# A fused attention and two-MLP kernel on one core: the second pass's attention starts earlier and is spread wider

## The chip, the cores and the metric

The kernel runs on one core of a Trainium2 chip. That core has a matrix engine (TensorE, PE in the profile), a vector engine (VectorE, DVE), a scalar engine (ScalarE, ACT), a GpSimd engine (POOL), and SyncE (SP), whose queue issues all the DMAs here. Each engine works through its own instructions strictly in order; a semaphore tells it when another engine's result is there. The metric is the device time of one execution in microseconds (us), lower is better.

## The reference

```python
kv  = einsum('bhsd,bhse->bhde', k, v)            # B, H, S, D = 8, 8, 576, 64
out = einsum('bhsd,bhde->bhse', q, kv)
x = out / sqrt(mean(out*out, -1) + 1e-6) * g_norm  # -> (4608 tokens, 512)
h = x @ w_in                                     # 512 -> 2048
x = (relu(h) + log1p(exp(-abs(h)))) @ w_out      # softplus, 2048 -> 512
h = max(x @ w1, x @ w2, x @ w3)                  # 512 -> 768
y = h @ w_out2                                   # 768 -> 512
```

Everything is float32. The attention has no softmax: for each batch a 64 x 64 matrix `kv` per head is made once and every query is multiplied by it; then each head's output is normalized.

## The kernel before

The 4608 tokens go through in five passes (`NS`: twice 464 tokens in each of the first four, twice 448 in the last). A pass holds its activations transposed, features on the partitions and tokens along the row, in two token halves. Every dense layer is worked as 2 x 2 block products with seven multiplications instead of eight (numbered 1, 5, 6, 2, 7, 4, 3 in their order of work); one "group" (`run_group`) is the seven products of one pair of weight rows, and each product is two matmuls of 128x128 by 128x464 (two records per matmul in the trace in the first pass, so four records a product).

The first pass multiplies in plain float32 and prepares the weights on the way: a raw block is loaded (`load_raw`, three buffers), turned into float32 by two ScalarE and two VectorE instructions (`rebase`, `join`; tiles `raw`, `cv`, `sw`), four sums of blocks are formed on GpSimd (`sums_of_weights`, `sw`), then each sum is split into a high and a low part (`make_unit`: ScalarE casts, GpSimd subtracts, tiles `u`, four buffers) and written to DRAM (`keep_first`, tiles `wd`) for the later passes. Those multiply three times with high and low parts (`mm3`).

Order is written by hand. Every step is put on a list with a time in "slots" (`at(t, fn, ...)`); one group is 7 slots. The list is sorted, and a scheduler keeps nearly this order on each engine; SyncE's order is pinned to it in this part. In the first pass, groups 0 to 7 are the first layer (`Xh`, `Yh`, `Wh` in PSUM), groups 8 to 15 the second layer (`Xx`, `Yx`, `Wx`; the last four, here called X20, X21, X30 and X31, start at slots 84, 91, 98 and 105), groups 16 to 24 the three-way layer (`Xo`, `Yo`, `Wo`; nine groups from `base2` = slot 119 on), and the output layer begins at slot 184. In the second layer every product is added to the running sums by VectorE (`x2`); in the three-way layer ScalarE first copies three or four products of a group out of PSUM (`m`), and the next product of the same bank cannot begin before that copy.

Beside the three-way layer runs the next pass's attention (`attention_beside`). For each of the two new batches, k and v of four head pairs are loaded (`load_kv`, two pairs of buffers), multiplied (`kv_mm`, `kvps`), and copied and split (`kv_evict`: `kvh`, `kvl`). Then come eight steps, one for each token half and head pair, numbered k = 0 to 7 here:

- `load_q` and `split_q`: `qh` by ScalarE, `ql` by GpSimd for even pairs and by VectorE for odd ones;
- `out_mm`: six short matmuls into `o`;
- `square`: on ScalarE the square `sq`, the scaled copy `og` and the cast `sh`; the low part `sl` again on GpSimd for even pairs, on VectorE for odd ones;
- `ssq_mm`: two matmuls `ss`, of `sh` and of `sl`, with a matrix of ones;
- `norm`: ScalarE `r`, `r`, `t`; VectorE `t`, `r`; GpSimd multiplies `og` by `r`.

At the end `combine_x` splits the eight `og` into the operands of the second pass (`hi`, `lo`).

Of the kernel before, what the change touches and what calls it, by code (L numbers as in the profile page):

```python
# [48 lines left out]
def kernel(  # L49
# [111 lines left out]
    def at(t, fn, *args):  # L161
        events.append((t, len(events), fn, args))
# [381 lines left out]
    rt, tt = {}, {}  # L544
# [98 lines left out]
    def new_batches(pas, t):  # L643

        a = TOK[pas] + t * NS[pas]
        first = -1 if a == 0 else (a - 1) // S
        return list(range(first + 1, (a + NS[pas] - 1) // S + 1))

    def attention_beside(pas, t0):

        n = NS[pas]

        for t, tt, dts in ((0, t0 - 9, (0, 2, 6, 9)), (1, t0 + 16, (0, 3, 6, 9))):
            for b in new_batches(pas, t):

                for p in range(NP):
                    at(tt + (dts[p] - 10 if p < 2 else dts[p - 2] + 0.15), load_kv, b, p)
                    at(tt + dts[p] + 0.1, kv_mm, b, p)
                at(tt + dts[3] + (0.2 if t == 0 else 1.35), kv_evict, b)
        for k in range(2 * NP):  # L660
            h, p = divmod(k, NP)
            a = TOK[pas] + h * n
            t = t0 + 8 + 6 * k
            at(t - 6, load_q, a, n, p)
            at(t - 3, split_q, a, n, p)
            at(t + 0.3, out_mm, a, n, p)
            at(t + 0.4, square, a, n, p)
            at(t + 4.8, ssq_mm, a, n, p)
            at(t + 4.9, norm, a, n, p)

    def run_pass(pas, base):
# [140 lines left out]
        if pas + 1 < NPASS:  # L812
            attention_beside(pas + 1, base2)
            for s, ms in enumerate(STEPS):
                at(base3 + 5 + SLOT[ms[-1]] + 0.5, combine_x, pas + 1, (s,))
# [87 lines left out]
    for k in range(-1, 2 * NP + 2):  # L903
        t = OPEN + 3 * (k + 1)
# [145 lines left out]
```

## Time and profile before

| | us |
|---|---|
| three runs, median (lowest to highest) | 1412.64 (1410.28 to 1413.76) |
| the profiled execution's own time | 1412.19 |
| its span, first to last instruction | 1410.4 |
| busy in the span: PE, DVE, ACT, POOL | 1388.8, 810.3, 747.2, 727.8 |

The profile's engines are PE, PEld (weight loads, which overlap PE), DVE, ACT, POOL and SP. A timeline row gives the start, the length, the engine, the line of the kernel, the operation and the tiles (written <- read), the shape, how many equal records were merged, and in brackets the idle time before it with the instruction that ended it. Instructions overlap a little at their ends, so the step from one start to the next is the better price where an engine is busy.

### The profile page before, as it was taken

What the parts mean: (1) busy time and instruction counts of PE and PEld (TensorE: products, weight loads), DVE (VectorE), ACT (ScalarE), POOL (GpSimd) and SP (SyncE); (2) the same over time, 40 slices, a digit from 0 to 9 for tenths busy, and PEclk for the clock granted to TensorE, in tenths of its full rate; (3) what the DMA queues carried; (4) which work ended last, traced back from release to release, by engine and by line L of the source; (5) the groups of instructions that cost most, each with busy time, mean ns of one, the idle gap of its engine ahead of it and who ended that gap; (6) DMA issues with size and microseconds to landing.
All of it is one profiled execution on the core that took longest, in us unless ns stands there. A gap on an engine that the chain in (4) does not pass through costs nothing.

```text
span 1410.4 us, 18509 instructions
## 1 busy us (share of the span) xinstructions
PE 1388.8 (98%) x6098; PEld 1111.6 (79%) x6098; DVE 810.3 (57%) x1283; ACT 747.2 (53%) x1427; POOL 727.8 (52%) x666
## 2 busy tenths in 40 slices
PE   8899999999999999999999999999999999999998
PEld 5344455544688888888888898888888889999898
DVE  5655566667355575764456567554475764456544
ACT  6766646665375545754543566464446754543332
POOL 3898787865364464544434444443364534444320
PEclk9999999999999999999999999999999999999999
DMA  7587778756699986667666875766676667666665
GB/s 278 188 285 277 275 273 329 248 196 210 222 321 332 316 306 214 213 206 267 209 209 209 268 247 188 258 221 209 209 218 208 212 200 269 220 214 210 211 219 180
DMA packets 122142, 336.51 MB, mean 239 GB/s; under 512 B 13120, under 2 KB 33472, under 8 KB 122048
## 3 DMA queue, kind: packets, MB, share of 16 engines
q1 hardware_dynamic: 122048, 335.33, 71.2%
q8 instruction: 49, 0.80, 0.2%
q14 instruction: 45, 0.37, 0.1%
HBM read 269.88 MB, written 65.40 MB: 238 GB/s over the span
## 4 chain that ended last, share of the span: by engine, by line
PE 87%; DMA 4%; ACT 3%; POOL 2%; DVE 2%; issue 1%; SPq 0%; POOLq 0%; ACTq 0%
PE Xo L136 4%; PE Xo L137 4%; PE Xo L138 4%; PE Xx L136 4%; PE Xx L138 4%; PE Xx L137 4%; PE Xh L136 4%; PE Xh L137 4%; PE Xh L138 4%; PE Xx L372 3%; PE Xo L372 2%; PE Xh L372 2%; PE Yo L138 2%; PE Yo L137 2%; PE Yo L136 2%; PE Yh L136 2%
## 5 line engine op out<-in xcount | busy, mean ns | idle before, releaser
L126 POOL TENSOR_TENSOR lo<-e,hi 128x464 fp32r<-128x464 f32 (+1 forms) x160 | 188.2, 1209 | 186.0 <-ACT hi L120 175.4
L120 ACT CAST hi<-t 128x464 fp32r<-128x464 f32 (+1 forms) x120 | 65.4, 545 | 118.3 <-DVE e L132 47.2
L126 POOL TENSOR_TENSOR u<-sw,u 128x512 fp32r<-128x512 f32 (+1 forms) x92 | 109.8, 1218 | 28.0 <-ACT u L120 27.9
L120 ACT COPY m<-Xo 128x464 f32<-128x464 f32 (+1 forms) x135 | 72.7, 544 | 82.5 <-PE Xo L138 73.9
L129 DVE TENSOR_TENSOR x<-x,Xx 128x464 f32<-128x464 f32 (+1 forms) x120 | 75.4, 631 | 55.5 <-PE Xx L138 51.2
L132 POOL TENSOR_TENSOR e<-e 128x464 f32<-128x464 f32 (+1 forms) x40 | 47.4, 1185 | 100.3 <-DVE t L132 93.2
L120 ACT CAST hi<-e 128x464 fp32r<-128x464 f32 (+1 forms) x160 | 85.0, 580 | 20.3 <-PE Yx L137 17.0
L126 DVE TENSOR_TENSOR lo<-t,hi 128x464 fp32r<-128x464 f32 (+1 forms) x120 | 75.7, 634 | 34.3 <-ACT hi L120 31.5
L136 PE MATMUL Xo<-hi,u 128*128 128x464 f32 (+1 forms) x224 | 84.7, 379 | 0.6 <-ACT m L120 0.5
L137 PE MATMUL Xo<-lo,u 128*128 128x464 f32 (+1 forms) x224 | 83.0, 370 | 0.0
L138 PE MATMUL Xo<-hi,u 128*128 128x464 f32 (+1 forms) x224 | 82.9, 370 | 0.0
L129 DVE TENSOR_TENSOR Wh<-h,Wh 128x464 f32<-128x464 f32 (+1 forms) x40 | 25.7, 641 | 96.3 <-PE Wh L138 70.3
L156 ACT ACTIVATE e<-h 128x464 f32<-128x464 f32 (+1 forms) x80 | 47.2, 591 | 61.4 <-DVE h L129 61.4
L126 POOL TENSOR_TENSOR lo<-m,hi 128x464 fp32r<-128x464 f32 (+1 forms) x40 | 47.7, 1209 | 56.4 <-ACT hi L120 54.1
L609 POOL TENSOR_TENSOR og<-og,r 128x464 f32<-128x464 f32 (+1 forms) x32 | 41.6, 1301 | 66.5 <-DVE r L605 60.1
L120 ACT COPY h<-Xh 128x464 f32<-128x464 f32 (+1 forms) x108 | 58.7, 543 | 31.4 <-PE Xh L138 25.1
L132 POOL TENSOR_TENSOR sw<-sw 128x256 f32<-128x256 f32 x84 | 66.4, 790 | 16.5 <-DVE sw L260 7.1
L137 PE MATMUL Xh<-lo,u 128*128 128x464 f32 (+1 forms) x194 | 72.2, 372 | 0.0
L136 PE MATMUL Xh<-hi,u 128*128 128x464 f32 (+1 forms) x194 | 72.1, 372 | 0.0
L138 PE MATMUL Xh<-hi,u 128*128 128x464 f32 (+1 forms) x194 | 71.8, 370 | 0.0
L136 PE MATMUL Xx<-hi,u 128*128 128x464 f32 (+1 forms) x192 | 71.4, 372 | 0.1
L129 DVE TENSOR_TENSOR h<-h,Yh 128x464 f32<-128x464 f32 (+1 forms) x80 | 50.5, 631 | 36.1 <-PE Yh L138 18.2
(268 smaller groups left out, 4155.3 us busy)
## 6 DMA issues: line engine op xcount, KB each, us to landing
u<-wd SPq DMA_DIRECT2D x241, 512.0 KB, 4.6
ux<-wd SPq DMA_DIRECT2D x99, 512.0 KB, 3.5
wd<-u SPq DMA_DIRECT2D x69, 512.0 KB, 6.4
u<-wd SPq DMA_DIRECT2D x104, 256.0 KB, 4.1
raw<-in_w_out_dram SPq DMA_DIRECT2D x22, 512.0 KB, 5.1
k<-in_kp_dram SPq DMA_DIRECT2D x31, 320.0 KB, 5.0
v<-in_vp_dram SPq DMA_DIRECT2D x31, 320.0 KB, 5.6
raw<-in_w_dram SPq DMA_DIRECT2D x18, 512.0 KB, 5.4
```

The lines of the kernel that those rows point to most:

```text
L120: nc.scalar.copy(hi, src)
L126: eng_lo.tensor_tensor(out=lo, in0=src, in1=hi.bitcast(F32), op=ALU.subtract)
L129: eng.tensor_tensor(out=o, in0=a, in1=b, op=ALU.add)
L132: eng.tensor_tensor(out=o, in0=a, in1=b, op=ALU.subtract)
L136: nc.tensor.matmul(acc, wh, xh, start=first, stop=False, skip_group_check=on)
L137: nc.tensor.matmul(acc, wh, xl, start=False, stop=False, skip_group_check=on)
L138: nc.tensor.matmul(acc, wl, xh, start=False, stop=last, skip_group_check=on)
L156: tables["used"].append(nc.scalar.activation(out, src, func, **kw).ins)
L372: nc.tensor.matmul(acc, w[:, c * P:(c + 1) * P], rhs[m, c], start=first and c == 0, stop=c == 1, skip_group_check=not first)
L609: nc.gpsimd.tensor_tensor(out=og, in0=og, in1=r, op=ALU.mult)
```

## The change

For the second pass alone (`pas == 1`, whose attention runs beside the first pass) two time formulas change. The first batch's k and v products move from `t0 - 9` to `t0 - 26.5`, the second batch's from `t0 + 16` to `t0 + 1`, where t0 is slot 119; and step k of the eight moves from `t0 + 8 + 6 k` to `t0 - 16 + 8.5 k`. So the steps stand at slots 103, 111.5, 120, 128.5, 137, 145.5, 154 and 162.5 where they stood at 127, 133, and so on to 169. No instruction of the computation is added or dropped.

```diff
+        early = pas == 1
-        for t, tt, dts in ((0, t0 - 9, (0, 2, 6, 9)), (1, t0 + 16, (0, 3, 6, 9))):
+        for t, tt, dts in ((0, t0 - (26.5 if early else 9), (0, 2, 6, 9)), (1, t0 + (1 if early else 16), (0, 3, 6, 9))):
             for b in new_batches(pas, t):
...
-            t = t0 + 8 + 6 * k
+            t = t0 + (-16 + 8.5 * k if early else 8 + 6 * k)
             at(t - 6, load_q, a, n, p)
             at(t - 3, split_q, a, n, p)
             at(t + 0.3, out_mm, a, n, p)
             at(t + 0.4, square, a, n, p)
             at(t + 4.8, ssq_mm, a, n, p)
             at(t + 4.9, norm, a, n, p)
```

Three places of the new order matter below. The first is TensorE between step 2's last `o` matmul and its `ss` matmuls. Before, in the middle of the three-way layer:

```order
L138 MATMUL o_1931<-qh_1872,kvl0_87 128x240
L372 MATMUL Xo_1949<-x2_734,sw_1784 128x464
L372 MATMUL Xo_1949<-x2_810,sw_1784 128x464
L372 MATMUL Yo_1956<-t1_1563,sw_1784 128x464
L372 MATMUL Yo_1956<-t1_1619,sw_1784 128x464
L468 MATMUL kvps_1856<-v_1863,k_1862 128x128 x5
L372 MATMUL Xo_1812<-t4_1565,sw_1687 128x464
L372 MATMUL Xo_1812<-t4_1621,sw_1687 128x464
L372 MATMUL Xo_1949<-t2_1564,sw_1784 128x464
L372 MATMUL Xo_1949<-t2_1620,sw_1784 128x464
L591 MATMUL ss_1994<-sh_1939,ones_84 128x464
L592 MATMUL ss_1994<-sl_1940,ones_84 128x464
```

After the change step 2 stands where the second layer has just ended:

```order
L138 MATMUL o_1746<-qh_1695,kvl0_87 128x240
L372 MATMUL Xo_1717<-t2_1630,sw_1624 128x464
L372 MATMUL Xo_1717<-t2_1708,sw_1624 128x464
L372 MATMUL Wo_1775<-x2_833,sw_1624 128x464
L372 MATMUL Wo_1775<-x2_900,sw_1624 128x464
L468 MATMUL kvps_1736<-v_1658,k_1657 128x128 x5
L591 MATMUL ss_1803<-sh_1754,ones_84 128x464
L592 MATMUL ss_1803<-sl_1755,ones_84 128x464
```

Four products and one k-v product stood between the two; now two products and one k-v product do.

The second place is GpSimd from the same step's `ql` to its `sl`. Before:

```order
L126 TENSOR_TENSOR ql_1873<-qraw_1817,qh_1872 128x464
L126 TENSOR_TENSOR u_1975<-sw_1784,u_1975 128x2x256
L126 TENSOR_TENSOR u_1991<-sw_1784,u_1991 128x2x256
L609 TENSOR_TENSOR og_1834<-og_1834,r_1892 128x464
L126 TENSOR_TENSOR lo_2579<-og_1834,hi_2578 128x464
L132 TENSOR_TENSOR sw_1907<-sw_1907 128x256
L129 TENSOR_TENSOR sw_1907<-sw_1907 128x256
L132 TENSOR_TENSOR sw_1907<-sw_1907 128x256 x2
L126 TENSOR_TENSOR sl_1940<-sq_1938,sh_1939 128x464
```

After:

```order
L126 TENSOR_TENSOR ql_1696<-qraw_1677,qh_1695 128x464
L132 TENSOR_TENSOR x2_839<-x2_866,x2_839 128x464
L126 TENSOR_TENSOR u3_1899<-sw_1702,u3_1899 128x256
L132 TENSOR_TENSOR t4_1709<-x2_900,t2_1708 128x464
L609 TENSOR_TENSOR og_1655<-og_1655,r_1684 128x464
L126 TENSOR_TENSOR lo_2575<-og_1553,hi_2574 128x464
L132 TENSOR_TENSOR sw_1796<-sw_1796 128x256
L126 TENSOR_TENSOR lo_2579<-og_1655,hi_2578 128x464
L129 TENSOR_TENSOR sw_1796<-sw_1796 128x256
L132 TENSOR_TENSOR sw_1796<-sw_1796 128x256 x2
L126 TENSOR_TENSOR sl_1755<-sq_1753,sh_1754 128x464
```

What stands between them has grown by two instructions in all: the operands of the three-way layer (`x2`, `t4`), the scaling of step 1 (`og`), two splits for the second pass (`lo`) and the sums of a weight block (`sw`) now lie in front of `sl`.

The third place is VectorE around step 1, whose `ql` and `sl` it makes. Before:

```order
L256 SCALAR_TENSOR_TENSOR cv_1839<-cv_1839,raw_1690 128x512
L602 SCALAR_TENSOR_TENSOR t_1795<-ss_1791,t_1795 128x464
L129 TENSOR_TENSOR m22_1805<-m22_1805,Yo_1713 128x464
L605 SCALAR_TENSOR_TENSOR r_1794<-t_1795,r_1794 128x464
L781 TENSOR_TENSOR m22_1696<-m22_1696,m22_1805 128x464
L260 SCALAR_TENSOR_TENSOR sw_1784<-raw_1690,cv_1839 128x2x256
L256 SCALAR_TENSOR_TENSOR cv_1904<-cv_1904,raw_1723 128x512
L126 TENSOR_TENSOR sl_1830<-sq_1828,sh_1829 128x464
```

After, at the end of the second layer (`t_1587` and `r_1586` belong to step 0):

```order
L126 TENSOR_TENSOR ql_1602<-qraw_1568,qh_1601 128x464
L605 SCALAR_TENSOR_TENSOR r_1586<-t_1587,r_1586 128x464
L129 TENSOR_TENSOR x2_810<-x2_810,Wx_1605 128x464
L129 TENSOR_TENSOR x2_763<-x2_763,Yx_1485 128x464
L260 SCALAR_TENSOR_TENSOR sw_1702<-raw_1493,cv_1699 128x2x256
L132 TENSOR_TENSOR t1_1629<-x2_763,x2_734 128x464
L129 TENSOR_TENSOR x2_866<-x2_866,Xx_1564 128x464
L132 TENSOR_TENSOR t2_1630<-x2_799,t1_1629 128x464
L129 TENSOR_TENSOR x2_866<-x2_866,Yx_1570 128x464
L256 SCALAR_TENSOR_TENSOR cv_1725<-cv_1725,raw_1627 128x512
L260 SCALAR_TENSOR_TENSOR sw_1702<-raw_1627,cv_1725 128x2x256
L126 TENSOR_TENSOR sl_1651<-sq_1649,sh_1650 128x464
```

The running sums `x2` and the operands `t1` and `t2` of the next layer now stand between and ahead of these.

## Rows read from the trace of the kernel before

**Rows 1.** The page, part 1: busy us, share of the span, instructions

```profile
PE 1388.8 (98%) x6098; PEld 1111.6 (79%) x6098; DVE 810.3 (57%) x1283; ACT 747.2 (53%) x1427; POOL 727.8 (52%) x666
```

**Rows 2.** Windows: second layer's end, three-way layer; length, busy by engine, clock, DMA

```profile
160.00:213.00 53.00, 53.00 (x152) 26.91 (x151) 33.47 (x52) 27.34 (x47) 41.37 (x42) 1.00 0.78 282
213.00:320.00 107.00, 101.11 (x332) 55.27 (x331) 66.98 (x100) 71.33 (x136) 80.30 (x78) 0.97 0.73 260
```

**Rows 3.** Waits of PE, 213 to 320: us in total, times, longest

```profile
PE Xo L372 <- ACT m L120: 4.2, 4, 3.0
PE ss L592 <- POOL sl L126: 1.6, 1, 1.6
```

**Rows 4.** Timeline of PE: the three gaps, and eight records at full speed

```profile
260.59 1.82 PE L372 MATMUL Xo<-t,sw 128*128 128x464 f32 x4 [0.74 <-ACT m L120]
...
264.21 0.48 PE L592 MATMUL ss<-sl,ones 128*128 128x464 f32 x1 [1.59 <-POOL sl L126]
...
269.43 3.28 PE L372 MATMUL Xo<-x,sw 128*128 128x464 f32 x8
...
284.88 6.35 PE L372 MATMUL Xo<-x,sw 128*128 128x464 f32 x8 [3.00 <-ACT m L120]
```

**Rows 5.** Timeline of ACT: a cast ahead of the late copy

```profile
279.74 0.62 ACT L120 CAST u<-sw 128x512 fp32r<-128x512 f32 x1 [2.05 <-POOL sw L129]
```

**Rows 6.** Timeline of PE: what one product, kvps, o and ss cost

```profile
209.31 1.28 PE L468 MATMUL kvps<-v,k 128*128 128x128 f32 x10
210.42 1.72 PE L372 MATMUL Xx<-e,sw 128*128 128x464 f32 x4
...
228.32 1.72 PE L372 MATMUL Yo<-t,sw 128*128 128x464 f32 x4
...
230.55 3.28 PE L372 MATMUL Xo<-t,sw 128*128 128x464 f32 x8
233.66 1.72 PE L372 MATMUL Wo<-x,sw 128*128 128x464 f32 x4
235.22 1.72 PE L372 MATMUL Yo<-x,sw 128*128 128x464 f32 x4
...
237.20 3.27 PE L372 MATMUL Xo<-x,sw 128*128 128x464 f32 x8
```

**Rows 7.** Timeline of POOL

```profile
212.38 1.57 POOL L132 TENSOR_TENSOR x<-x,x 128x464 f32<-128x464 f32 x1
...
234.60 1.18 POOL L126 TENSOR_TENSOR sl<-sq,sh 128x464 fp32r<-128x464 f32 x1
...
251.71 1.18 POOL L126 TENSOR_TENSOR ql<-qraw,qh 128x464 fp32r<-128x464 f32 x1
...
256.49 1.57 POOL L609 TENSOR_TENSOR og<-og,r 128x464 f32<-128x464 f32 x1
...
259.89 0.73 POOL L132 TENSOR_TENSOR sw<-sw 128x256 f32<-128x256 f32 x1
...
262.99 1.17 POOL L126 TENSOR_TENSOR sl<-sq,sh 128x464 fp32r<-128x464 f32 x1
```

**Rows 8.** Timeline of ACT: a query split and the start of a norm

```profile
250.02 0.58 ACT L120 CAST qh<-qraw 128x464 fp32r<-128x464 f32 x1
250.50 0.65 ACT L156 ACTIVATE r<-ss,epsc 128x464 f32<-128x464 f32 x1
251.18 0.59 ACT L156 ACTIVATE r<-r 128x464 f32<-128x464 f32 x1
251.80 0.59 ACT L601 ACTIVATE t<-r 128x464 f32<-128x464 f32 x1
```

**Rows 9.** Waits of SP's queue, 130 to 320: us in total, times, longest

```profile
SPq L459 <- PE kvps L468: 9.9, 2, 8.6
```

**Rows 10.** Timeline of DVE: the same instruction at two places

```profile
234.98 1.30 DVE L126 TENSOR_TENSOR ql<-qraw,qh 128x464 fp32r<-128x464 f32 x1 [6.00 <-ACT qh L120]
...
313.10 0.64 DVE L126 TENSOR_TENSOR ql<-qraw,qh 128x464 fp32r<-128x464 f32 x1 [4.43 <-ACT qh L120]
```

## The prediction

> **What bounds the kernel now.** I read the busy times first, then the stages, then TensorE's waits stage by stage, then the queues of the engines it waits for. TensorE is busy for 98% of the span [rows 1], so only a stretch where it is not busy can give anything back, and the change touches the stretch from the end of the second layer to the end of the three-way layer. In the windows, TensorE is busy for all 53 us of the second layer's end, and for 101.11 of the 107 us of the three-way layer; the granted clock there is 0.97 in the mean, and 1.00 before [rows 2]. So 5.89 us are idle. Two kinds of wait make them: a `Xo` product behind ScalarE's copy `m`, 4.2 us, and one `ss` behind GpSimd's `sl`, 1.6 us [rows 3]. The timeline puts them at three places: 0.74 us at 260.6, 1.59 us at 264.2 and 3.00 us at 284.9, and the eight records behind the last one took 6.35 us where eight others took 3.28 [rows 4]. That is the lower of TensorE's two clock levels (1.2 instead of 2.4 GHz) after a 3 us pause, and costs 3.07 us more. In all the stage loses 5.89 + 3.07 = 9.0 us, 0.6% of the time, and no gain in this stage can be larger.
>
> Why the copies are late: ScalarE works in order, and at 279.7, five microseconds ahead of the end of the longest gap, a cast `u` of a weight sum had waited 2.05 us for GpSimd [rows 5]. GpSimd is busy for 80.30 of the 107 us, and ScalarE for 71.33 [rows 2]; an attention step loads both, and eight steps stood in this stage.
>
> **What is removed there.** Steps 0 and 1 leave the three-way layer, and the other six stand 8.5 slots apart. GpSimd and ScalarE get a quarter less attention work, the sums of weights are formed earlier relative to the products that need them, and the copies no longer stand behind a late sum. I book all 9.0 us as gone in the old places, and 0.2 us as what is left of such waits; the bounds for what is left are 0 and 3.1, the last one 3.00 us wait again.
>
> **What is moved, and its price in TensorE time.** Nothing is added: TensorE's own work is the same. One product (four records) takes 1.56 us, from 230.55 to 233.66 for two. One `kvps` takes 1.11 (209.31 to 210.42); the six `o` matmuls 230.55 - 228.32 - 1.56 = 0.67; the two `ss` 237.20 - 235.22 - 1.56 = 0.42 [rows 6]. Each is the same work in another place, so the sum of them is unchanged, and only new waits count. I follow them in order of time.
>
> *The second layer.* Here products are added up by VectorE, not copied by ScalarE, and ScalarE is busy for 27.34 of 53 us [rows 2]; so what it does for steps 0 and 1 lies beside other work and costs nothing. The first batch's k and v are loaded ten slots ahead of their products, some 15 us at 1.56 us a slot. Zero.
>
> *Step 1, where the second layer ends (A).* Between its `o` and its second `ss` TensorE has one and a half products, 2.3 us. Beside them ScalarE has `sq`, `og` and `sh`, three instructions of about 0.58 us [rows 8], and VectorE `sl`, 0.64 [rows 10]: together 2.4. But VectorE's `sl` now stands behind eleven others from `ql` on. Bounds: 0 when they have all run, and 2.5 us when four of them still stand ahead. I take 0.7, one instruction ahead, because most of them are sums that follow each product as it ends.
>
> *Step 2, where the three-way layer begins (C).* This is the main price. From the end of step 1's `ss`, TensorE has until step 2's `ss`: half a product, `Xo` and `Yo`, a `kvps`, the six `o`, two products, a `kvps`: 4.5 x 1.56 + 2 x 1.11 + 0.67 = 9.9 us [rows 6]. Beside it runs a chain that nothing shortens: ScalarE takes step 1's `r`, one weight cast, `r`, `t`, and then step 2's `qh`, 0.65 + 0.58 + 0.59 + 0.59 + 0.58 = 3.0 us [rows 8] with the cast priced as `qh`. Then GpSimd works its queue from `ql` to `sl` in order: `ql` 1.18, `x2` 1.57, `u3` 0.73 (same size as one `sw`), `t4` 1.18 (as `ql`), `og` 1.57, two `lo` of 1.18, four `sw` of 0.73, `sl` 1.17, which makes 12.7 us [rows 7]. The chain is 15.7 us long, TensorE's work 9.9: it waits 5.8 us. A second way to it: before, the same step's queue ran from 251.71 to 264.16, 12.5 us [rows 7], and TensorE lost 0.74 + 1.59 us beside it [rows 4]; now two products fewer stand between its `o` and its `ss`, 3.1 us of cover that is gone, and the queue is 0.2 longer: 5.6. I take 5.8. Bounds: 1.6 us, the `sl` wait of before, if TensorE is itself held up in front of step 2; and 7.4 if the weight cast stands another 1.6 us for its sum on GpSimd.
>
> *The clock after it (D).* The one row on this says that a pause of 3.00 us was followed by 3.07 us of loss [rows 4]. A pause of 5.8 us should be followed by the lower level too, but some of it may pass while TensorE still waits. Bounds 0 and 3.1; I take 2.3, near the row.
>
> *SyncE's queue.* Loads of k and v wait for the buffers of the pair two before, so for a product of TensorE; one such wait took 8.6 us before and held up everything queued behind it [rows 9]. It now comes with the second batch, at slots 120 and 123, and raw weight blocks and the writes of `u` stand behind it. The raw block directly behind it belongs to a group that begins at slot 140, some 25 us later, so I book nothing; no wait of TensorE in the three-way layer names what stood behind the 8.6 us of before [rows 3].
>
> **The sum.** 0.7 + 5.8 + 2.3 + 0.2 = 9.0 us of new losses against 9.0 us of old ones: no change. The profiled execution took 1412.19 us for a span of 1410.4, and the median of the runs is 1412.64; I forecast 1412.4, between the two, and the times below are counted from it.
>
> **A rule that speaks against the change.** VectorE's `ql` took 1.30 us at 235.0 and 0.64 us at 313.1 [rows 10]; in the first case GpSimd's `sl` ran from 234.60 to 235.78 [rows 7]. The Trainium skill, page "SBUF — State Buffer", section "Who interferes with whom", says that a VectorE instruction with two inputs in SBUF and a GpSimd instruction that reads SBUF share an interface, and that the later one is blocked until the other ends. By that rule the trace's two numbers agree, and it would make the second rival.
>
> **The rivals.**
>
> 1. *The wait of step 2 is hidden: faster.* If TensorE reaches step 2 late, because a sum on VectorE or a copy holds it, GpSimd has run part of its queue already. With C at its lower bound, 1.6, and no pause long enough for the lower clock, the new losses are 0.7 + 1.6 + 0.2 = 2.5 against 9.0, 6.5 us less: 1405.9. For it: GpSimd was busy for only 41.37 of 53 us in the second layer's end [rows 2]. Against: the chain from step 1's `ss` to step 2's `sl` is one of dependences and of queue order, and it is as long as said however early GpSimd was free. Chance 0.30.
> 2. *VectorE and GpSimd hold each other up at the layer's end: slower.* Five of VectorE's twelve instructions around step 1 have both inputs in SBUF (`ql`, `r`, `t1`, `t2`, `sl`). If each one meets GpSimd as at 235.0, `sl` comes 5 x 0.66 = 3.3 us later. A is then 3.3 and C 7.4, each with a spell at the lower clock, 2 x 3.1: 16.9 + 0.2 against 9.0, so 1420.5. It decides where three or more of the five meet. For it: GpSimd is the busiest of the three helpers there. Against: one meeting costs 0.66 only, and TensorE's waits of before name VectorE nowhere [rows 3]. Chance 0.12.
> 3. *The old waits stay.* If the late sums come from the chain that prepares weights and not from attention, the 3.00 us wait and its spell at the lower clock, 6.1 us, stay with the new ones: 1418.3. For it: the cast ahead of the late copy waited for a weight sum, no attention tile [rows 5]. Against: in the new order six steps stand in the time of eight, and TensorE comes later by the wait of step 2, which lets the preparation get ahead. Chance 0.08.
>
> **How the numbers follow.** The forecast case (within 0.3%, that is within 4.2 us, about what a measurement here can tell from no change) has 0.50, and its own range, from new losses between 4.8 and 13.2 us, is 1408.2 to 1416.6. Rival 1 is faster by over 0.3%, rivals 2 and 3 slower by over 0.3%: 0.30 and 0.20. For 8 times in 10 the range goes down through most of rival 1 and up to between rivals 3 and 2: 1405 to 1418.
>
> **What would show it.** Right: in the changed profile TensorE waits 4 to 7 us in the first 20 us of the three-way layer, most of it an `ss` behind GpSimd's `sl` and ScalarE's `sh`, followed by a stretch at half clock; after it the waits for copies `m` are under 1 us in all. Wrong in C: no `ss` wait over 2 us there. Wrong in what is removed: waits for `m` of over 2 us later in the layer. Wrong in the place: a wait of TensorE in the second layer, for k and v or for VectorE's sums.

## The result and the profile after

The changed kernel took 1419.67 us in the median of four executions (1418.0 to 1422.33), the kernel before 1412.04 beside it: a ratio of 1.006, 95% interval 1.0048 to 1.0072. It is 0.6% slower; the forecast of no change was wrong, and the time lies above the range.

The page's first part, of the changed kernel, answers to [rows 1]:

```profile
PE 1390.9 (98%) x6098; PEld 1113.6 (79%) x6098; DVE 811.5 (57%) x1283; ACT 746.7 (53%) x1427; POOL 727.6 (51%) x666
```

The span grew from 1410.4 to 1417.9. TensorE has the same instructions, yet is busy 2.1 us longer; how much of that is lower clock is not separated, since the kernel before has a spell too [rows 4]. The other 5.4 us are idle time. The two windows, as in [rows 2], hold 5.0 of it:

```profile
160.00:213.00 53.00, 52.31 (x168) 27.88 (x166) 28.91 (x47) 28.29 (x51) 39.51 (x41) 1.00 0.92 328
213.00:320.00 107.00, 96.83 (x297) 51.83 (x298) 67.53 (x98) 68.44 (x131) 81.33 (x78) 0.95 0.64 219
```

Idle time is 0.69 in the first and 10.17 us in the second, where it was nothing and 5.89. TensorE's waits from 213 to 320, beside [rows 3]:

```profile
PE ss L592 <- POOL sl L126: 4.4, 3, 3.0
PE ss L591 <- ACT sh L120: 2.0, 1, 2.0
PE Xx L372 <- DVE x L129: 2.0, 1, 2.0
PE o L137 <- POOL ql L126: 1.4, 2, 1.1
PE Yo L372 <- DVE m L782: 0.4, 1, 0.4
PE Xo L372 <- ACT m L120: 0.3, 1, 0.3
```

The copies `m` cost 0.3 us instead of 4.2: the old losses did go. What came stands in TensorE's timeline, the gaps answering to [rows 4]:

```profile
222.26 3.27 PE L372 MATMUL Xx<-t,sw 128*128 128x464 f32 x4 [2.00 <-DVE x L129]
...
232.45 0.37 PE L137 MATMUL o<-ql,kvh 128*128 128x224 f32 x1 [0.36 <-POOL ql L126]
...
239.54 0.76 PE L591 MATMUL ss<-sh,ones 128*128 128x464 f32 x1 [2.03 <-ACT sh L120]
243.29 0.76 PE L592 MATMUL ss<-sl,ones 128*128 128x464 f32 x1 [3.00 <-POOL sl L126]
...
299.52 0.42 PE L137 MATMUL o<-ql,kvh 128*128 128x336 f32 x1 [1.06 <-POOL ql L126]
...
307.74 0.48 PE L592 MATMUL ss<-sl,ones 128*128 128x464 f32 x1 [0.87 <-POOL sl L126]
...
313.32 1.82 PE L372 MATMUL Yo<-t,sw 128*128 128x464 f32 x4 [0.43 <-DVE m L782]
```

There are three places. The first, at 222, is step 1's: an `Xx` product of the second layer, no attention matmul, waits for a sum on VectorE. The second, from 232 to 243, is step 2's, the price C of the prediction. The third, from 299 on, belongs to step 6. Two spells at the lower clock go with the first two, as the windows show (columns as above; the clock is the third number from the end):

```profile
222.00:226.00 4.00, 3.73 (x5) 1.66 (x6) 3.97 (x6) 2.45 (x6) 4.00 (x4) 0.57 0.47 131
...
239.00:246.00 7.00, 3.46 (x5) 1.79 (x6) 0.27 (x1) 3.33 (x8) 5.38 (x7) 0.54 0.97 342
```

**Why step 1's place waits.** VectorE's timeline shows it:

```profile
216.60 0.64 DVE L602 SCALAR_TENSOR_TENSOR t<-ss,t 128x464 f32<-128x464 f32 x1 [0.99 <-ACT t L601]
217.16 0.63 DVE L126 TENSOR_TENSOR ql<-qraw,qh 128x464 fp32r<-128x464 f32 x1
217.71 1.71 DVE L605 SCALAR_TENSOR_TENSOR r<-t,r 128x464 f32<-128x464 f32 x1
219.34 0.62 DVE L129 TENSOR_TENSOR x<-x,Wx 128x464 f32<-128x464 f32 x1
...
221.59 0.62 DVE L129 TENSOR_TENSOR x<-x,Xx 128x464 f32<-128x464 f32 x1
222.13 1.27 DVE L132 TENSOR_TENSOR t<-x,t 128x464 f32<-128x464 f32 x1
...
225.20 0.97 DVE L126 TENSOR_TENSOR sl<-sq,sh 128x464 fp32r<-128x464 f32 x1
```

Step 0's norm (`t`, `r`) stands in front of the running sums. VectorE waited 0.99 us for ScalarE's `t`, and `r` took 1.71 us where the same line took 0.72 at 220.30 in the run shifted by three slots below: GpSimd's `u` lay over it.

```profile
217.63 1.29 POOL L126 TENSOR_TENSOR u<-sw,u 128x512 fp32r<-128x512 f32 x1 [1.38 <-ACT u L120]
```

That `u` ended at 218.92, and `r` 0.50 later. The Trainium skill, page "SBUF — State Buffer", section "Who interferes with whom", says that of a VectorE instruction with two SBUF inputs and a GpSimd instruction that reads SBUF the later one is blocked; the trace agrees. Together the 0.99 and about 1.0 are the 2.00 us; this is a sum of rows, and no run takes one of the two away alone. Two more of VectorE's instructions met GpSimd right behind: `t` at 222.13 (beside GpSimd's `x`, 221.74 to 222.91) took 1.27 us, and step 1's `sl` at 225.20 (beside GpSimd's `t`, 224.50 to 225.67) 0.97, where `ql` at 217.16, of the same size, took 0.63.

**Why step 2 waits.** GpSimd's queue from `ql` to `sl`, beside [rows 7], and ScalarE's in front of `sh`:

```profile
230.80 1.60 POOL L126 TENSOR_TENSOR ql<-qraw,qh 128x464 fp32r<-128x464 f32 x1
...
235.70 1.16 POOL L609 TENSOR_TENSOR og<-og,r 128x464 f32<-128x464 f32 x1
236.82 1.18 POOL L126 TENSOR_TENSOR lo<-og,hi 128x464 fp32r<-128x464 f32 x1
...
238.65 1.18 POOL L126 TENSOR_TENSOR lo<-og,hi 128x464 fp32r<-128x464 f32 x1
...
242.08 1.16 POOL L126 TENSOR_TENSOR sl<-sq,sh 128x464 fp32r<-128x464 f32 x1
```

```profile
236.90 0.58 ACT L120 CAST hi<-og 128x464 fp32r<-128x464 f32 x1 [4.15 <-POOL og L609]
...
237.94 0.54 ACT L581 ACTIVATE sq<-o 128x464 f32<-128x464 f32 x1
...
238.91 0.58 ACT L120 CAST sh<-sq 128x464 fp32r<-128x464 f32 x1
```

From 230.80 to 243.24 the queue takes 12.4 us (predicted 12.7). ScalarE is stuck too: the cast `hi` for the second pass stands in front of `sq` and waits 4.15 us for GpSimd's `og`. But `sh` was ready at 239.49, 2.6 us before GpSimd came to `sl`, so the end of step 2's wait is set by GpSimd's queue alone.

**Why step 6 waits.** GpSimd again, in order behind the weight preparation. Sums that waited for VectorE's join stand in front of `sl`, whose `sh` was ready at 303.18. A `u` that waited for ScalarE's cast stands in front of `ql`, but it explains only 0.4 of the 1.06 us: ScalarE ended `qh`, which `ql` reads, at 297.91, and `ql` began at 298.27.

```profile
297.04 1.28 POOL L126 TENSOR_TENSOR u<-sw,u 128x512 fp32r<-128x512 f32 x1 [1.59 <-ACT u L120]
298.27 1.19 POOL L126 TENSOR_TENSOR ql<-qraw,qh 128x464 fp32r<-128x464 f32 x1
...
304.21 0.73 POOL L132 TENSOR_TENSOR sw<-sw 128x256 f32<-128x256 f32 x1 [1.97 <-DVE sw L260]
...
306.52 1.17 POOL L126 TENSOR_TENSOR sl<-sq,sh 128x464 fp32r<-128x464 f32 x1
```

It resembles [rows 5]: the three helpers hand weight blocks to each other, and what stands in line behind such a handing over is late.

### The profile page after: what moved, and what is told of

Its sections match the earlier page's. It is cut to its first block, busy times and chain, and to the rows that moved or that the text cites. A ratio compares the mean times of both kernels' runs of the same rounds, so it can differ in the third digit from the quotient of the medians.

```text
span 1417.9 us, 18498 instructions
## 1 busy us (share of the span) xinstructions
PE 1390.9 (98%) x6098; PEld 1113.6 (79%) x6098; DVE 811.5 (57%) x1283; ACT 746.7 (53%) x1427; POOL 727.6 (51%) x666
## 4 chain that ended last, share of the span: by engine, by line
PE 85%; DMA 4%; POOL 3%; DVE 2%; ACT 2%; issue 2%; SPq 1%; POOLq 0%; DVEq 0%; ACTq 0%
PE Xo L136 4%; PE Xo L138 4%; PE Xo L137 4%; PE Xh L136 4%; PE Xx L136 4%; PE Xh L137 4%; PE Xx L138 4%; PE Xh L138 4%; PE Xx L137 4%; PE Xx L372 3%; PE Yo L138 2%; PE Yo L136 2%; PE Xh L372 2%; PE Yo L137 2%; PE Yx L136 2%; PE Yx L138 2%
## 5 line engine op out<-in xcount | busy, mean ns | idle before, releaser
L136 PE MATMUL Xx<-hi,u 128*128 128x464 f32 (+1 forms) x192 | 71.4, 372 | 0.0
L138 PE MATMUL Xx<-hi,u 128*128 128x464 f32 (+1 forms) x192 | 71.1, 370 | 0.0
```

The costliest lines, as they stand in the source:

```text
L136: nc.tensor.matmul(acc, wh, xh, start=first, stop=False, skip_group_check=on)
L138: nc.tensor.matmul(acc, wl, xh, start=False, stop=last, skip_group_check=on)
```

## The experiments

Theory Q says that the loss is made by the order inside the helpers' queues, at the handover from layer to layer; theory S that it is the price of starting early and spreading, wherever the steps fall. Each time stands with its ratio to the kernel before, run beside it on the same chip (medians 1411.6 to 1412.2). "Less" counts medians from the changed kernel's 1419.67, whose own interval is some 1.7 us to either side, so differences of one or two microseconds between edited kernels tell nothing. A profile shows one execution, which can lie 2 us off the median.

**One part alone: the first k and v early.**

```diff
-            t = t0 + (-16 + 8.5 * k if early else 8 + 6 * k)
+            t = t0 + 8 + 6 * k
```

(against the changed kernel; and the second batch back at `t0 + 16`)

> The kernel before with one part of the change alone: the first batch's k and v come at t0 - 26.5; the second batch and all eight steps stay where they were. Theory Q (the loss is made at the handover, in the queues of GpSimd and ScalarE around steps 1 and 2): no step moves, so the time is that of the kernel before, 1412 us, within 0.3%. Theory L (the earlier loads and copies of k and v crowd the weight preparation in the second layer; the first batch's landing was followed by waits for kvh and kvl): 2 to 4 us slower, 1414 to 1416. Theory S (attention steps beside the second layer cost, whichever the instruction): 1412 as well, since no step is there.

1413.4, ratio 1.0014 (1.0005 to 1.0023): 1.2 us. Theory L was too high; most of the loss needs the steps. The old waits are there as before:

```profile
PE Xo L372 <- ACT m L120: 4.5, 4, 3.0
```

**The early splits held back** (`combine_x` of the second pass ordered behind all that is issued ahead of it on ScalarE and GpSimd).

```diff
+        if late(fn, args):
+            with after(newest()):
+                fn(*args)
```

> The changed kernel, but the two splits for the second pass (two hi casts on ScalarE, two lo subtractions on GpSimd, of the og of steps 0 and 1) that stood in front of step 2's squares are kept behind the work of the three-way layer. Theory Q: ScalarE no longer waits 4.15 us for og ahead of step 2's sq, and GpSimd's queue is 2.4 us shorter: of step 2's 6.7 us of loss and the 1.3 us of half clock after it some 5 go: 1414 to 1416. Theory S: step 2 waits for its own chain (norm of step 1, qh, ql) anyway, or the time is lost in the next step: within 1.5 us of 1419.7.

1416.12, ratio 1.0027 (1.0018 to 1.0036), 3.5 us less. The wait for ScalarE's `sh` is gone, that for `sl` stays. But from the product behind step 2's `o` to this `ss` it is 8.0 us instead of 10.2, close to the two `lo` (2.4 us) that left GpSimd's queue:

```profile
239.15 0.74 PE L592 MATMUL ss<-sl,ones 128*128 128x464 f32 x1 [3.43 <-POOL sl L126]
```

**Step 2's `sl` on VectorE.**

```diff
-        split(nc.scalar, sq, sh, sl, nc.vector if p % 2 else nc.gpsimd)
+        split(nc.scalar, sq, sh, sl, nc.vector if p % 2 or a == TOK[1] and p == 2 else nc.gpsimd)
```

> The changed kernel with one instruction moved: step 2's sl is made by VectorE instead of GpSimd. Theory Q: the 3.00 us wait of the second ss for GpSimd goes, the 2.03 us wait of the first ss for ScalarE's sh stays, and the half-clock spell may stay or shrink: 1415.5 to 1417. Theory S: VectorE is as crowded as GpSimd there, or the time comes back in the next step: 1418.5 to 1420.

1415.01, ratio 1.002 (1.0011 to 1.0029), 4.7 us less for one instruction moved. In its profile the wait for `sh` is as it was, and the clock from 213 to 255 is 1.00. With `sl` out of GpSimd's queue the wait for it shrank to 0.37. So GpSimd's line sets the end of C, and ScalarE's `hi` costs something of its own, 2.02 us, only where `sl` is out of that line.

```profile
236.48 0.48 PE L591 MATMUL ss<-sh,ones 128*128 128x464 f32 x1 [2.02 <-ACT sh L120]
237.33 0.48 PE L592 MATMUL ss<-sl,ones 128*128 128x464 f32 x1 [0.37 <-DVE sl L126]
```

**Step 2 four slots later** (step 3 stays at `t0 + 9.5`, where it was).

```diff
+            t = t0 + ((-16, -7.5, 5, 9.5, 18, 26.5, 35, 43.5)[k] if early else 8 + 6 * k)
```

> The changed kernel with step 2 four slots (6.2 us) later, at t0 + 5, and step 3 one slot earlier instead of at 9.5 exactly where it was; all else as changed. Theory Q: step 2's chain from step 1's norm has 6.2 us more cover, as long as its loss of 6.7: step 2's wait and the half clock after it go, 8 us in all: 1411 to 1413. Theory S: the waits move to step 3, which now stands 4.5 slots behind step 2: 1417 to 1420.

1413.76, ratio 1.0014 (1.0005 to 1.0023), 5.9 us less. Neither `ss` of step 2 waits any more; its `o` waits 1.81 for `ql`, which is why it is not 8. C is settled: place and queue, as predicted. In this profile the `Xx` product still waits 2.00 us (at 220.30), but at full speed behind it, so the 5.9 hold some of A's lower clock too.

**Step 0's norm six slots later.**

```diff
-            at(t + 4.9, norm, a, n, p)
+            at(t + 4.9 + (6 if early and k == 0 else 0), norm, a, n, p)
```

> The changed kernel with one part moved: the norm of step 0 (ScalarE's r, r, t; VectorE's t and r; GpSimd's og) comes six slots later, so on VectorE its t and r stand behind the sums x of the second layer's last products instead of in front of them. Theory A (VectorE in order: step 0's late t and its r of 1.71 us held the running sum that the Xx product at 222.26 waited for): the 2.00 us wait for x and the half-clock spell behind it (1.5 us) go, 3 to 4 us in all: 1415.5 to 1417. Rival: the sum is late anyway, or the time comes back at step 2, in front of whose ql GpSimd's og of step 0 now stands: 1418.5 to 1420.5.

1416.1, ratio 1.0036 (1.0023 to 1.005), 3.6 us less. The `Xx` product waits 0.20 instead of 2.00 us and runs at full speed, though 3.03 us appear in front of step 2, whose `ql` now has step 0's `og` ahead of it, which takes 1.56 us (its two `ss` waits shrink to 1.04). Step 1's own `ss` now waits 0.96 us for `sl`:

```profile
218.05 1.82 PE L372 MATMUL Xx<-t,sw 128*128 128x464 f32 x4 [0.20 <-DVE x L129]
...
222.02 0.48 PE L592 MATMUL ss<-sl,ones 128*128 128x464 f32 x1 [0.96 <-DVE sl L126]
...
231.39 0.55 PE L137 MATMUL o<-ql,kvh 128*128 128x224 f32 x1 [3.03 <-POOL ql L126]
```

**Step 6's `ql` and `sl` on VectorE** (both splits, as above, for `(a, p) == (TOK[1] + NS[1], 2)`).

> The changed kernel with step 6's ql and sl made by VectorE instead of GpSimd. Theory Q for the late waits too (GpSimd's queue of u and sums of weights stands in front of ql and sl): the waits of 1.06 us at 299.5 and 0.87 us at 307.7 go: 1417.5 to 1418.2. Rival (the chain that prepares weights sets the pace there, and TensorE waits for it in another place): 1419 to 1420.

1419.53, ratio 1.0057 (1.0044 to 1.0069): nothing. Theory Q's number failed here; VectorE is as full as GpSimd (both busy 46.4 of the 65 us from 255 to 320), and its own sums `m` came late instead:

```profile
300.63 1.79 PE L372 MATMUL Yo<-t,sw 128*128 128x464 f32 x4 [1.41 <-DVE m L129]
...
313.73 1.79 PE L372 MATMUL Yo<-t,sw 128*128 128x464 f32 x4 [1.54 <-DVE m L782]
```

**All four edits** (step 2 later; `ql` and `sl` of steps 2 and 6 on VectorE; step 0's norm later).

> The changed kernel with the edits together: step 2 at t0 + 5, ql and sl of steps 2 and 6 on VectorE, the norm of step 0 six slots later. Theory Q with A: the gains add up, 5.9 (measured with step 2 later alone) + 1.8 (step 2's remaining wait for ql) + 3.5 + 1.9 = 13 us: 1406 to 1409, faster than the kernel before. Theory S (the steps beside the second layer and the handover cost about the same wherever they stand): the waits come back elsewhere, 1412 to 1415.

1413.31, ratio 1.0011 (1.0003 to 1.002). This is in theory S's range: the gains did not add up. At the handover no wait is over 1 us; late in the layer the wait of 1.41 us behind step 6 on VectorE stands as in the run before, here with the lower clock behind it (3.43 us for four records).

**The whole early schedule three slots later** (`-13 + 8.5 * k`; k and v at `t0 - 23.5` and `t0 + 4`).

> The changed kernel with its whole early schedule three slots (4.7 us) later: k and v, and all steps, at -13 + 8.5 k; the spacing as changed. Theory Q (the loss comes from where steps 1 and 2 fall against the handover's queue): step 2 stands behind x2 and t4, not among them, so most of the 8 us goes, though step 1 comes nearer to the handover: 1412 to 1416. Theory S (start beside the second layer and the spacing cost, not the place): 1418 to 1421.

1419.23, ratio 1.0053 (1.004 to 1.0066): no gain, as theory S had it. But the trace has Q's mechanism at new places: step 1 stands in the handover now, where ScalarE has a weight block's `cv` and `u`, which waited 3.38 and 1.04 us, in front of its `sq`; and on GpSimd an `og`, a `lo`, four `sw` and a `u` stand between step 2's `ql` and `sl`.

```profile
228.37 0.48 PE L591 MATMUL ss<-sh,ones 128*128 128x464 f32 x1 [2.51 <-ACT sh L120]
...
245.84 0.48 PE L592 MATMUL ss<-sl,ones 128*128 128x464 f32 x1 [2.90 <-POOL sl L126]
```

So the time alone did not tell Q from S here; the rows did.

**No attention beside the layers.**

```diff
+            if early:
+                at(t - 1, load_og, a, n, p)
+                continue
```

> The changed kernel without the second pass's attention: no k and v products, no q splits, o, squares, ss or norms; q itself is loaded in the place of each step's scaled result. What is left beside the second and the three-way layer is the weight preparation. The work left out on TensorE is eight steps of 0.67 + 0.42 us and eight k-v products of 1.11 us, 17.6 us. Theory Q (waits come from attention's instructions in the queues): the waits go too, those of before as well, 1412.0 - 17.6 - 9.0 = 1385.5, within 2. Theory W (the weight preparation alone makes waits of some size): 1389 to 1394.5.

1386.73, ratio 0.9821 (0.9805 to 0.9837), within theory Q's 1385.5 ± 2. The weight preparation alone leaves hardly a wait (155 to 335 us; two more are of 0.2 each):

```profile
PE Xo L372 <- ACT m L120: 0.5, 1, 0.5
PE Xx L372 <- DVE x L129: 0.3, 1, 0.3
```

With the 17.6 us left out put back, 1404.3 is an estimate of what any placement can reach, if nothing but the waits changes.

**One part alone: only steps 0 and 1 early** (with the first k and v; the second batch at `t0 + 16`).

```diff
+            t = t0 + ((-16, -7.5)[k] if early and k < 2 else 8 + 6 * k)
```

> One part of the change alone: the first batch's k and v and steps 0 and 1 early, as changed; the second batch and steps 2 to 7 where they stood before (six slots apart). Theory Q: what steps 0 and 1 cost early (1.5 and 4.0 us) comes, what step 2 costs at the handover (8 us) does not; if the old waits (9.0 us) belong to steps 2 to 5 in their old places, they stay: 1416 to 1418. If two steps fewer in the layer are enough to take the old waits away, as the prediction had it: 1408 to 1410.

1417.1, ratio 1.0037 (1.0024 to 1.0049): theory Q's number. Two steps fewer in the layer did not remove the waits for `m`. The longest (2.71 us at 293.6) stands behind the same `Wo` product as the 3.00 of before, the fifth of the layer; two others (0.70 and 2.24) stand around the first `Wo`, where there was none:

```profile
PE Xo L372 <- ACT m L120: 5.8, 4, 2.7
PE Xx L372 <- DVE x L129: 2.8, 1, 2.8
```

**Step 2 later and step 0's norm later, nothing moved between engines.**

> The changed kernel with step 2 at t0 + 5 and the norm of step 0 six slots later; nothing moved between engines. Alone the two gave 5.9 and 3.6 us. If gains add: 1410.2, a little faster than the kernel before. If what one removes comes back at the other's place: 1412.5 to 1414.

1413.09, ratio 1.0015 (1.0005 to 1.0025). They do not add: step 0's `og` stands in front of step 2's `ql`, and the wait for it, 1.81 with step 2 later alone, is 2.14; `Yo` and `Xo` products wait another 0.8 us for VectorE's `t`; and each of the two, alone, had already taken the lower clock at 222 with it. That these make up all that is missing (2.9 us) is not shown.

**Three edits** (step 2 at `t0 + 5` on VectorE, step 0's norm later, step 6 on GpSimd at `t0 + 37`).

> As with all four edits, but step 6 is on GpSimd again and two slots later, at t0 + 37: step 2 at t0 + 5 with ql and sl on VectorE, the norm of step 0 six slots later. All four together left, late in the layer, a wait of 1.41 us for VectorE's m behind step 6's ql and r, with half clock after it (1.6 us). Theory Q: these 3 us go and no more than 1 comes back at step 6's new place: 1410 to 1411.5. Theory W (the weight preparation sets the pace at the layer's end): 1412.5 to 1414.

1410.88, ratio 0.9994 (0.9986 to 1.0003): no difference from before can be told. Step 6's two waits shrank to one of 0.74; no wait is over 1 us (the longest is step 1's `ss`, 0.96):

```profile
294.46 0.42 PE L137 MATMUL o<-ql,kvh 128*128 128x336 f32 x1 [0.74 <-POOL ql L126]
```

**Seven slots apart, none early** (from the old start, and three slots earlier; the second batch's k and v at `t0 + 20` and `t0 + 17`).

```diff
+            t = t0 + 8 + (7 if early else 6) * k
```

> The kernel before with the steps seven slots apart instead of six, from t0 + 8 as before (the last at t0 + 57), the second batch's k and v at t0 + 20; no step is early. Theory Sp (spacing takes the old waits): of 5.9 us idle and the half clock in its wake most goes, 1405 to 1408. Theory P (places decide): at this phase each step meets a group at the same point, and the waits repeat or vanish together: either under 1407 or over 1414.

> As seven apart at 8, but all steps three slots earlier against the groups (from t0 + 5, the last at t0 + 54; second batch at t0 + 17). Theory Sp: the same time as at 8, within 2 us, 1405 to 1408. Theory P: more than 3 us from the run at 8.

From `t0 + 8`: 1408.24, ratio 0.9972 (0.9961 to 0.9983), faster than both kernels, by 3.8 and 11.4 us, and just outside the ranges of both theories. From `t0 + 5`: 1411.41, ratio 0.9994 (0.9986 to 1.0003). The first has lost the old `m` waits; the second has one nearly as long as the longest of [rows 4], at another place:

```profile
300.34 1.82 PE L372 MATMUL Yo<-t,sw 128*128 128x464 f32 x4 [1.11 <-DVE m L782]
```

```profile
276.49 3.33 PE L372 MATMUL Xo<-t,sw 128*128 128x464 f32 x4 [2.90 <-ACT m L120]
```

The first row is the longest wait at `t0 + 8`, where the clock stayed at 1.00; the second that at `t0 + 5`. The spacing is the same and the times are 3.2 us apart, with intervals that do not meet: the place against the groups matters (theory P), not the spacing alone. A spacing of 8.5 slots with no step early was not run.

**Three edits, and besides the splits held back and step 1's `ss` and norm one slot later.**

> The run with three edits (1410.9), and besides the two early splits for the second pass kept behind the three-way layer, and step 1's ss and norm one slot later. Theory Q: the 0.96 us wait of step 1's ss goes, the queues at the handover are 2.4 us shorter, which no wait there still needs: 1409 to 1410.5. Rival: the splits collect in the output layer and delay it: 1411 to 1413.

1411.12, ratio 0.9993 (0.9984 to 1.0001), as without: the rival's number, but its reason is not seen (TensorE's waits from 345 us on are 2.0 us in all, 1.6 with three edits). Step 1's wait fell from 0.96 to 0.17, and others of 0.4 to 0.8 came. Repaired, the early schedule equals the kernel before; I found no place at which it is better.

## Why the prediction was wrong, step by step

- **What is removed (9.0 us, bounds 0 to 3.1 left).** The old waits are gone from the changed profile, so the booking held, but not its reason: with steps 0 and 1 early and the others in their old places, waits for `m` of 5.8 us were there, half of them at old places and half at new ones. They go or stay with the places. And 3.07 of the 9.0 was a spell at the lower clock in one execution. The mean clock of that execution is 0.998; of 94 later ones of the kernel before, 50 have 0.999 or more. The 20 at 1.000 have a median of 1411.0, the 12 at 0.997 or less 1412.4. The spell is not always there to be won back.
- **The second layer (zero).** Step 0 waited 0.18 and 0.51 us there in the changed kernel's profile; in the profiles of nine edited kernels it waited at neither place: about right for step 0. The wait of `Xx` for a sum, which falls in the second layer's last group, belongs to A.
- **A (0.7, bounds 0 to 2.5): the step that failed first.** I priced only what waits for step 1's `sl`, and that price was near: in eight edited kernels the `ss` waits 0.96 or 0.97 us for it (in the changed kernel's profile it does not wait, since the lower clock had made TensorE later). I wrote that eleven instructions stand ahead of `sl` and did not ask who waits for those: they are running sums, which TensorE needs at once when the layer ends, and step 0's late norm stood in front of them. That wait was 2.0 us, the lower clock behind it 1.5. It is the sign that the prediction itself named for a wrong place, a wait for VectorE's sums in the second layer. With the norm moved, 3.6 us went, a net figure: step 2's waits fell too, and the 0.96 came.
- **C (5.8, bounds 1.6 to 7.4): right.** 0.36 + 2.03 + 3.00 = 5.4 us. ScalarE's `hi`, which I had not seen, made the first `ss` late, but not the second, which ended the wait.
- **D (2.3): mis-sized.** The eight records from 243.84 took 4.54 us instead of 3.28, 1.3 us; with the `ss` in front of them about 1.5.
- **Left late in the layer (0.2): failed.** Step 6's waits and two for `m` are 1.06 + 0.87 + 0.43 + 0.30 = 2.7 us. GpSimd's weight preparation stood in front of `sl`, and ScalarE's `qh` came late for `ql`. Moving the work to VectorE moved the wait; two slots' difference in place (with the other edits) left 1.4 us.
- **SyncE's queue (zero).** The view of SyncE's waits from 130 to 320 has 13.8 us for products of k and v where [rows 9] had 9.9; no wait of TensorE over 0.1 us in that stretch names a DMA. With the first k and v early and no step moved, 1.2 us were lost; through which wait stays open.

```profile
SPq L459 <- PE kvps L468: 13.8, 4, 6.3
```

- **The rivals.** Rival 1 failed, though its condition came true: TensorE was held up in front of step 2 by a sum on VectorE, but the chain of C starts at step 1's `ss`, so it came later too, and C stayed 5.4. Rival 2 (1420.5, chance 0.12) came nearest in time and in form: a second wait at the layer's end with its own half-clock spell. Its condition was met: three of the five instructions met GpSimd, `r` (1.71 us), `t2` (1.27, the `t` at 222.13) and `sl` (0.97). But together they lost 2.0 us and not 3.3; only the 1.0 of `r` reached TensorE in this profile, and C did not grow to 7.4. Where the clock had not fallen, `t2` and `sl` account for what the `ss` waits: with step 0's norm later they took 1.28 and 0.97, 1.0 us more than 0.63 each, and the wait is 0.96. Rival 3 is refuted: in the changed profile the waits for `m` are 0.3 us, and without attention the weight preparation leaves 1.2 us.

In sum, by the rows of the two profiles: A cost 2.8 us more than booked (3.5), the end of the layer 2.5 and the second layer 0.7; C and D cost 0.4 and 0.8 less. So the new losses are 13.8 us against 9.0 of old ones, 4.8 of the 7.5 by which the span grew. Another 1.6 us were lost before anything that the change moves: the first `Xh` product began 1.41 us later, and at 153 us the lag was 1.56.

```profile
32.13 1.72 PE L372 MATMUL Xh<-og,sw 128*128 128x464 f32 x4
```

```profile
33.54 1.72 PE L372 MATMUL Xh<-og,sw 128*128 128x464 f32 x4
```

The first row is the kernel before, the second the changed one. In the 17 profiles of this case this start lies between 32.13 and 33.72, and the change moves nothing that runs ahead of it, so it is put down to the executions; what it does to the medians is not known. About 1 us is not separated. The parts do not add exactly either: removed together, A and C gave 6.6 us, not 3.6 + 5.9.

## What to carry to other kernels

Before an attention step (or any chain over three in-order engines) is put at another place, list on each engine not only what delays the step but who needs the instructions that will now stand behind it; where one layer hands over to the next, those are needed at once. In this kernel work split over in-order engines is priced by its place, so try two or three phases against the loop's period before judging a spacing: the same spacing gave 1408.2 and 1411.4. And do not book a clock loss seen in one execution as if every execution had it.

## What the hardware showed unexpectedly

Gaps of about the same length were followed by the lower clock in one execution and not in another: after the 2.00 us gap at 222.26 four records took 3.27 us, after one of 1.75 in the run with `sl` on VectorE (219.22) and one of 2.00 with step 2 later (220.30) they took 1.82. With step 6 on VectorE the same `Yo` product waited 1.41 us in two kernels, and its four records then took 1.79 us in one and 3.43 in the other (all four edits). What decides between them is not settled by these runs.
